# Attention and token mixing on one core: neighbouring heads paired, 128-row loads, and a preparation in which TensorE sums weight halves, pools k and turns q and k of batch 0

## The chip, the core and the metric

The kernel runs on one core of a Trainium2 chip. The metric is the device time in microseconds (us) of one execution. Before the change it is 653.0 us, the median of three runs (652.75 to 656.43). The engines are called as the profile calls them: PE (TensorE, matrix products), PEld (PE's weight loads), DVE (VectorE), ACT (ScalarE), POOL (GpSimd) and SP (SyncE, which issues the transfers here).

## The reference, cut to what matters

```python
# q, k, v: (8 batches, 8 heads, 576 tokens, 64); all float32
k_p = k.reshape(8, 8, 72, 8, 64).mean(axis=3)      # 576 tokens pooled to 72
v_p = v.reshape(8, 8, 72, 8, 64).mean(axis=3)
scores = 0.125 * q @ k_p.transpose(0, 1, 3, 2)
attn = softmax(scores)                             # sum + 1e-9 as divisor
x = concat_heads(attn @ v_p)                       # (8, 576, 512)

theta = x @ w_theta                                # 512x512
zr, zi = x * cos(theta), x * sin(theta)
y = w_tok_r @ zr + w_tok_i @ zi                    # 576x576 each, over the tokens
u = x + y
out = u + relu(u @ w_ch)                           # 512x512
```

The four weights (`moe_w_theta`, `moe_w_tok_r`, `moe_w_tok_i`, `moe_w_ch`) are stored as float64, and the kernel reads them as pairs of 32-bit words. q, k, w_theta and w_tok_i are scaled by 8 in the inputs.

## The kernel before, in words

**Streams and the schedule.** All work is written as small generators, the streams, each of which does one step (a transfer, a multiplication, a copy) between two `yield`s. `SCHEDULE` is a table of 1,882 words written by hand. The kernel walks through it and takes one step of the stream that the word names: `S1.3v` is one step of the stream S1.3, and a letter v, g or a at the end says that DVE, POOL or ACT does it (`pick()` returns the letter). Each engine runs its instructions in the order of the words, so a step that waits holds up everything behind it on its engine.

**Number formats.** A product with weights is made three times in PE's float32r format: each matrix is split into a high part (rounded to float32r) and a low part (the rest), and high x high, low x high and high x low are added in one bank of PSUM. Names in h and l are such pairs: th/tl (w_theta), WTh/WTl (token weights, transposed), chh/chl (w_ch), zh/zl, uh/ul, xh/xl, eh/er (attention).

**Weights.** `to_f32` (L268 to L296) makes float32 from the two words of a float64: seven elementwise steps, the last of which adds the high part t and the small rest s on the engine that the letter names. `channel_weights` (streams h for w_theta, c for w_ch) loads 128 rows in two transfers of 64 (L308, the rows in the order of the paired heads), converts them, and splits the sum into two parts (the low one at L328). `token_weights` (streams w) do the same for 128 rows of w_tok_r or w_tok_i, into one of three buffers `t`; `turn_weights` (W) transposes the blocks of 128x128 on PE (L379, L388, L389) and splits them into WTh and WTl.

**One batch.** The streams of batch b, in the order in which its work flows:
- k, v: loads. K, V: sums over 8 tokens, on DVE and POOL (`pool_sum`, L405 and L410); only v of batch 0 is summed on PE (`pool_on_pe`, L459 and L461), which then holds the sums in PSUM.
- K (`keys`): transposes of the pooled k (L469, L477), copied into kpT.
- Q (`queries`): half of the heads per step, four transfers (L496) that bring blocks of 32 columns, then one stream transpose on DVE (L503).
- S (`soften`, five tiles of 128 tokens): scores on PE (L580), maximum on DVE (L610), exponential on ACT (L618), normalised weights en (L641, L650). Two heads share one multiplication. From batch 2 on, the turned attention weights come back through 32 transfers per batch (L725).
- X: attention times v on PE (L772) into xT. T (five tiles): x is split into xh and xl (xl at L788), theta on PE (L795, bank pt), cosine and sine and the products on ACT and DVE (L799 to L832, L801 and L824 among them), and a transpose of x on PE (L805, px).
- Z: z split into zh and zl (L846). M (`mix`): y on PE (L859), u on DVE (L865). F (`final`): the closing multiplication on PE (L887), ReLU and sum on DVE (L893), and the transfers out.

M and F work on the 576 tokens in two halves of `HALF = S // 2` = 288. Tokens and channels meet in pairs of heads c and c + 2 of each group of four, so the channel order inside the kernel isn't that of the output, and the weights' rows and columns are loaded and split by views that undo this:

```python
    def rows_paired(w):
        return w.rearrange("(j h c d) n -> j c h d n", j=2, h=2, c=2)
```

What decides who waits is thus three things: the table's order on each engine, the landing of the transfers, and how soon a buffer is free again. `EARLY` is 2 (the first two batches turn their attention weights on PE), `V_ON_PE` is 1.

## Time and profile before

| Profiled execution | |
|---|---|
| its time | 655.2 us |
| its span | 653.4 us |
| mean granted TensorE clock | 0.968 |
| PE busy | 593.4 us (91%), 3,891 instructions |
| PEld busy | 544.5 us (83%) |
| DVE busy | 498.2 us (76%), 987 |
| ACT busy | 315.4 us (48%), 675 |
| POOL busy | 303.8 us (47%), 342 |
| chain that ended last | PE 56%, DVE 21%, ACT 9%, DMA 4%, SP's queue 4% |
| DMA | 57.82 MB, 243,991 packets, 232,032 of them under 512 bytes |

The runs without a profile took 656.43, 652.75 and 653.0 us. The share of busy time is a mean over the whole span: PE is busy for 91% of it, yet the first slices of the page show it at 0 to 5 tenths. The preparation (weights, attention of batches 0 and 1) takes about the first 100 us; after it, mixing of one batch runs beside the attention of the next. An instruction's row gives start, duration, engine, line, output<-inputs, and in brackets what ended the wait before it.

### The profile page before, as it was taken

The numbers are of one execution on the slowest core, as the hardware profiler recorded it, in microseconds if no ns is written. First come the engines' busy times: TensorE is split into PE (matmuls) and PEld (weight loads), VectorE is DVE, ScalarE is ACT, GpSimd is POOL, SyncE is SP. The second block draws the span as 40 slices with busy tenths as digits, with TensorE's granted clock in tenths as the row PEclk, the third lists the DMA queues.
The fourth block names the chain that finished last, engine by engine and source line by source line (L and its number), as shares of the span: only waits on it lengthen the run. The fifth ranks groups of instructions, "written<-read, shape, count | busy, mean of one in ns | idle before, by whom it ended". The sixth has DMA issues, their size and how long they took to land.

```text
span 653.4 us, 11040 instructions
## 1 busy us (share of the span) xinstructions
PE 593.4 (91%) x3891; PEld 544.5 (83%) x3891; DVE 498.2 (76%) x987; ACT 315.4 (48%) x675; POOL 303.8 (47%) x342
## 2 busy tenths in 40 slices
PE   0567988999779989999999999999999999999996
PEld 0444568998569988999899989997999989999996
DVE  3879898898687798868898787788877898556424
ACT  2485574767682446424852565316642473155010
POOL 3122342145656856566355474746524516332640
PEclk9985888999989999999999999999999999999999
DMA  9995311247456524826354236641455031402204
GB/s 187 210 246 146 99 42 34 65 87 146 105 96 129 109 59 92 153 39 131 66 104 73 74 73 122 109 93 28 96 90 108 12 62 27 78 1 37 38 1 73
DMA packets 243991, 57.82 MB, mean 88 GB/s; under 512 B 232032, under 2 KB 232544, under 8 KB 243936
## 3 DMA queue, kind: packets, MB, share of 16 engines
q1 hardware_dynamic: 243936, 57.11, 44.2%
q8 instruction: 31, 0.51, 0.3%
q14 instruction: 24, 0.20, 0.1%
HBM read 37.81 MB, written 9.44 MB: 72 GB/s over the span
## 4 chain that ended last, share of the span: by engine, by line
PE 56%; DVE 21%; ACT 9%; DMA 4%; SPq 4%; issue 3%; POOL 2%; DVEq 0%; ACTq 0%; POOLq 0%
PE py L859 27%; PE pf L887 11%; PE pt L795 9%; PE pv L772 5%; PE s L580 3%; SPq L725 2%; DVE mx L610 2%; DMA WTh_st<-in_moe_w_theta_dram 2%; DVE g L801 1%; DVE z L824 1%; PE px L805 1%; ACT g L820 1%; DVE e L625 1%; DVE oT L893 1%; DVE eraw L746 1%
## 5 line engine op out<-in xcount | busy, mean ns | idle before, releaser
L859 PE MATMUL py<-WTh,zh 128*128 128x288 f32 x576 | 88.2, 300 | 1.3 <-DVE xT L865 0.7
L859 PE MATMUL py<-WTl,zh 128*128 128x288 f32 x576 | 88.1, 298 | 0.0
L859 PE MATMUL py<-WTh,zl 128*128 128x288 f32 x576 | 86.9, 298 | 0.0
L859 PEld LDWEIGHTS py<-WTh,zh 128*128 128x128 f32 x576 | 81.3, 192 | 2.3 <-DVE zh L175 1.0
L859 PEld LDWEIGHTS py<-WTl,zh 128*128 128x128 f32 x576 | 81.2, 191 | 0.1
L859 PEld LDWEIGHTS py<-WTh,zl 128*128 128x128 f32 x576 | 79.8, 190 | 0.6 <-DVE xT L865 0.2
L865 DVE TENSOR_TENSOR xT<-py,xT 128x288 f32<-128x288 f32 x64 | 28.5, 448 | 43.5 <-PE py L859 43.0
L580 PE MATMUL s<-kpT,qT 128*128 128x144 f32 (+1 forms) x320 | 49.6, 301 | 6.5 <-DVE e L625 3.2
L872 POOL TENSOR_TENSOR ul<-xT,uh 128x288 fp32r<-128x288 f32 x36 | 31.9, 893 | 45.0 <-ACT uh L173 36.3
L580 PEld LDWEIGHTS s<-kpT,qT 128*128 128x128 f32 (+1 forms) x320 | 43.8, 190 | 9.7 <-issue 3.7
L795 PE MATMUL pt<-th,xh 128*128 128x512 f32 x160 | 47.1, 417 | 3.6 <-ACT xh L173 1.2
L846 POOL TENSOR_TENSOR zl<-z,zh 128x1152 fp32r<-128x1152 f32 x14 | 38.4, 2744 | 23.7 <-ACT zh L173 23.1
L173 ACT CAST uh<-xT 128x288 fp32r<-128x288 f32 x32 | 13.6, 430 | 72.0 <-DVE xT L865 72.0
L795 PE MATMUL pt<-th,xl 128*128 128x512 f32 x160 | 45.4, 407 | 2.8 <-POOL xl L788 2.8
L887 PE MATMUL pf<-uh,chh 128*128 128x288 f32 x256 | 46.6, 304 | 1.2 <-DVE oT L893 1.2
L887 PE MATMUL pf<-ul,chh 128*128 128x288 f32 x256 | 44.8, 295 | 0.1
L799 ACT ACTIVATE g<-pt,c_magic 128x512 f32<-128x512 f32 x38 | 26.1, 687 | 38.8 <-PE pt L795 32.6
L795 PE MATMUL pt<-tl,xh 128*128 128x512 f32 x160 | 44.8, 403 | 0.0
L629 ACT ACTIVATE e<-e 128x576 f32<-128x576 f32 (+1 forms) x30 | 20.6, 686 | 50.0 <-DVE e L625 49.8
L788 POOL TENSOR_TENSOR xl<-xT,xh 128x512 fp32r<-128x512 f32 x26 | 34.2, 1319 | 22.3 <-ACT xh L173 11.7
L887 PE MATMUL pf<-uh,chl 128*128 128x288 f32 x256 | 44.3, 295 | 0.0
L795 PEld LDWEIGHTS pt<-th,xl 128*128 128x128 f32 x160 | 31.2, 196 | 10.6 <-POOL xl L788 3.6
(224 smaller groups left out, 1395.9 us busy)
## 6 DMA issues: line engine op xcount, KB each, us to landing
qsst<-in_q_dram SPq DMA_DIRECT2D x60, 144.0 KB, 3.3
out_dram<-R SPq DMA_DIRECT2D x112, 72.0 KB, 2.0
kpst<-in_k_dram SPq DMA_DIRECT2D x30, 256.0 KB, 4.0
vpst<-in_v_dram SPq DMA_DIRECT2D x28, 256.0 KB, 3.9
eraw<-G SPq DMA_DIRECT2D x96, 60.0 KB, 2.1
eraw<-G SPq DMA_DIRECT2D x96, 40.0 KB, 2.0
WTh_st<-in_moe_w_theta_dram SPq DMA_DIRECT2D x8, 256.0 KB, 7.8
wcraw<-in_moe_w_ch_dram SPq DMA_DIRECT2D x8, 256.0 KB, 4.0
```

The lines of the kernel that those rows point to most:

```text
L173: nc.scalar.copy(out, src)
L580: nc.tensor.matmul(scs[c // 2][:n, 2 * SP * (c % 2) : 2 * SP * (c % 2 + 1)], qT[:, c, t0 : t0 + n], kpT[:, c, :], start=True, stop=True,)
L629: nc.scalar.activation(e[:n], e[:n], AF.Exp, scale=scale)
L772: nc.tensor.matmul(pv[:, :gn], l, r, start=i == 0, stop=i == len(terms) - 1)
L788: ENG[pick()].tensor_tensor(xl, xT[:, :, o], f32(xh), ALU.subtract)
L795: nc.tensor.matmul(pt, l[:, c, :], r[:, c, :], start=i == 0, stop=i == 11)
L799: nc.scalar.activation(g, pt, AF.Identity, bias=c_magic)
L846: ENG[pick()].tensor_tensor(zl, z[:, :, o], f32(zh), ALU.subtract)
L859: nc.tensor.matmul(py[:, :HALF], l[:, kk, :], r[:, kk, t], start=i == 0, stop=i == 3 * NK - 1)
L865: nc.vector.tensor_tensor(u, py[:, :HALF], u, ALU.add)
L872: ENG[pick()].tensor_tensor(ul[:, c, t], u, f32(uh[:, c, t]), ALU.subtract)
L887: nc.tensor.matmul(pv[:, :HALF], l[:, kk, o], uhl[r][:, kk, t], start=i == 0, stop=i == 11)
```

## The change

Four things are changed in the preparation and one in the later loops; the schedule is rewritten throughout.

1. **Neighbouring heads are paired** (heads 2c and 2c + 1 in column block c). The inner channel order is then that of the output. Weights are loaded 128 rows at a time in one transfer instead of two of 64, k in loads of 128 rows of the flattened pools; the small part of en is one multiplication instead of two; the q of batches 1 to 7 comes in 8 transfers per half instead of 4.
2. **float64 halves are summed on PE.** `to_f32` leaves the high part t and the small rest `last` apart. For w_theta PE multiplies both by an identity into one bank (L316 and L317), and the two scaled parts th and tl are read from there. For the token weights the transpose of t and a product of `last` with the identity (`turned`) meet in the bank of the turned block. The sums for w_ch stay elementwise. The token weights have two buffers for t and two for `last`, and one for the step between.
3. **Batch 0's k is pooled on PE** (`K_ON_PE = 1`) and copied out of the bank.
4. **Batch 0's q is loaded by tokens**, in five tiles, and transposed on PE (`queries_on_pe`, `Q_ON_PE = 1`), then copied to qT.
5. **M and F cut the 576 tokens at 256** (256 and 320) instead of 288 and 288.

```diff
-    HALF = S // 2
+    PARTS = ((0, 256), (256, 320))
...
+    identr = const([P, P], F32R, "identr")
+    nc.vector.tensor_copy(identr, ident)
...
     def to_f32(raw, t, s, last=None):
...
-        nc.vector.scalar_tensor_tensor(s, lo.bitcast(U32), step, s, ALU.mult, ALU.mult)
-        yield
-        if scale:
-            nc.vector.scalar_tensor_tensor(t, t, scale, s, ALU.mult, ALU.add)
-        else:
-            ENG[pick()].tensor_tensor(t, t, s, ALU.add)
+        last = s if last is None else last
+        nc.vector.scalar_tensor_tensor(last, lo.bitcast(U32), 2.0**-52, s, ALU.mult, ALU.mult)
         yield
...
@@ channel_weights @@
-        for hh in range(2):
-            nc.sync.dma_start(raw[64 * hh : 64 * hh + 64], rows_paired(w)[c // 2, c % 2, hh])
+        nc.sync.dma_start(raw, w[P * c : P * c + P])
...
+        sum_ = bank([P, DM], *bank_of(c))
+        nc.tensor.matmul(sum_, ident, t, start=True, stop=False)
+        nc.tensor.matmul(sum_, identr, last, start=False, stop=True)
+        yield
+        if pick() == "a":
+            nc.scalar.activation(hi[:, c, :], sum_, AF.Copy, scale=scale)
+        else:
+            nc.vector.tensor_scalar(hi[:, c, :], sum_, scale, None, ALU.mult)
+        yield
+        nc.vector.scalar_tensor_tensor(
+            lo[:, c, :], sum_, scale, f32(hi[:, c, :]), ALU.mult, ALU.subtract
+        )
...
@@ token_weights @@
-            wbufs["t"] = [wa[:, 0 : 2 * S], wa[:, 2 * S :], wb[:, 0 : 2 * S]]
-            wbufs["s"] = [wb[:, 2 * S : 3 * S], wb[:, 3 * S :], wc]
+            wbufs["t"] = [wa[:, 0 : 2 * S], wa[:, 2 * S :]]
+            wbufs["s"] = [wb[:, 0 : 2 * S], wb[:, 2 * S :]]
...
@@ turn_weights @@
+        def turned(out, rows, cols):
+            t, s = wts[m]
+            nc.tensor.matmul(
+                out, t[rows, cols], ident[rows, rows], is_transpose=True, start=True, stop=False
+            )
+            nc.tensor.matmul(out, s[rows, cols], identr[rows, rows], start=False, stop=True)
...
-                    nc.tensor.transpose(pt[:, i - i0, :], src[:, P * i : P * i + P], ident)
+                    turned(pt[:, i - i0, :], every, slice(P * i, P * i + P))
...
+    def queries_on_pe(b, m):
...
+        nc.sync.dma_start(
+            st[:n].rearrange("p (h d) -> p h d", d=D),
+            q[b, :, t0 : t0 + n].rearrange("h s d -> s h d"),
+        )
+        yield
+        pq = bank([P, NC, P], "tp" if m % 2 else "px", f"pq{b}_{m}")
+        for c in range(NC):
+            nc.tensor.transpose(pq[:, c, :n], st[:n, P * c : P * c + P], ident[:n, :n])
+        yield
+        copy(pick(), qTs[b][:, :, t0 : t0 + n], pq[:, :, :n])
...
-        t = slice(HALF * hf, HALF * hf + HALF)
+        t0, n = PARTS[hf]
+        t = slice(t0, t0 + n)
```

The table of the schedule begins differently:

```diff
-k0.0 K0.0v K0.0g k0.2 K0.2g k0.1 K0.1v K0.1v K0.1g w0.0 w0.0 w0.0 w0.0 K0.0g K0 w0.0 w0.0 h0 h2 h0 h2 h0 h0 h2
+k0.0 w0.0 w0.0 w0.0 w0.0 w0.0 k0.1 K0.0 K0.0v h0 h0 h1 K0.1 K0.1a K0 K0a h0 h0 h0 h0 h0 h0 h0v h2 h2 h2 Q0.0
```

How it moves the instructions is shown at three places. In the rows, a line number is that of the kernel in question (the lines from 300 on have moved by 4 to 43), the names are those of the program with a running number at the end, and x4 stands for four like instructions in a row.

First PE at the very start of the program. Before:

```order
L469 MATMUL pk0_120<-ident_66,kp0_99 64x128 x4
L477 MATMUL pkr0_147<-ident_66,kpr0_104 64x64
L580 MATMUL s0_0_171<-kpT_82,qT0_151 128x144 x4
L580 MATMUL s0_1_0_197<-kpT_82,qT0_151 128x144 x2
L580 MATMUL s0_1_1_198<-kpT_82,qT0_151 128x144 x2
L459 MATMUL pvp0_228<-early_95,ident_66 128x128 x16
L461 MATMUL pvp0_228<-vprst0_246,ident_66 64x64 x8
L580 MATMUL s0_2_264<-kpT_82,qT0_151 128x144 x4
```

And PE at the same place now (kpp0 is the bank of the pooled k, ths0 that of the summed w_theta, pq0 that of a tile of q):

```order
L483 MATMUL kpp0_110<-kpst0_0_98,ident_66 128x128 x8
L483 MATMUL kpp0_110<-early_97,ident_66 128x128 x8
L494 MATMUL pk0_137<-ident_66,kp0_119 64x128 x4
L316 MATMUL ths0_150<-WTh_st_122,ident_66 128x512
L317 MATMUL ths0_150<-WTl_st_125,identr_71 128x512
L544 MATMUL pq0_0_160<-ident_66,qsst0_0_158 128x128 x4
L485 MATMUL kpp0_110<-kprst0_168,ident_66 64x64 x8
L504 MATMUL pkr0_179<-ident_66,kpr0_120 64x64
L623 MATMUL s0_0_182<-kpT_84,qT0_157 128x144 x4
L544 MATMUL pq0_1_197<-ident_66,qsst0_0_158 128x128 x4
```

Ahead of the first scores there now stand the pooling of k, the sum of the first tile of w_theta and the transposes of one tile of q; each tile of scores follows its own tile of q instead of all of q.

Second, POOL while the tiles of batch 1 are rotated (xl1_3 is the low part of the fourth tile of x of batch 1, kpst3_0 the first load of k of batch 3, whose sum is kp3). Before:

```order
L788 TENSOR_TENSOR xl1_2_1693<-xT1_1283,xh1_2_1692 128x512
L405 TENSOR_TENSOR kpst3_0_1653<-kpst3_0_1653 128x2x256
L405 TENSOR_TENSOR kpst3_0_1653<-kpst3_0_1653 128x2x128
L410 TENSOR_TENSOR kp3_1721<-kpst3_0_1653 128x128
L788 TENSOR_TENSOR xl1_3_1728<-xT1_1283,xh1_3_1727 128x512
L175 CAST xh1_4_1741<-xT1_1283 128x512
L788 TENSOR_TENSOR xl1_4_1742<-xT1_1283,xh1_4_1741 128x512
```

And POOL now:

```order
L826 TENSOR_TENSOR xl1_2_1698<-xT1_1359,xh1_2_1697 128x512
L409 TENSOR_TENSOR vpst2_1_1720<-vpst2_1_1720 128x2x256
L409 TENSOR_TENSOR vpst2_1_1720<-vpst2_1_1720 128x2x128
L414 TENSOR_TENSOR vp2_1529<-vpst2_1_1720 128x128
L175 COPY xT1_1359<-xT1_1359 128x4x64
L826 TENSOR_TENSOR xl1_3_1712<-xT1_1359,xh1_3_1711 128x512
L175 CAST Vh_88<-vp2_1529 64x4x64 x2
L577 TENSOR_TENSOR Vl_856<-vp2_1529,Vh_88 64x4x64 x2
L409 TENSOR_TENSOR kpst3_0_1815<-kpst3_0_1815 128x2x256
L409 TENSOR_TENSOR kpst3_0_1815<-kpst3_0_1815 128x2x128
L414 TENSOR_TENSOR kp3_1705<-kpst3_0_1815 128x128
```

The low part of the fourth tile stands ahead of the sum of batch 3's first k load instead of behind it; between the third and the fourth tile there stands now a sum of v of batch 2.

Third, PE at that place (pt is theta, px the transposed x, s2 scores of batch 2, pf0 the closing multiplication of batch 0). Before:

```order
L795 MATMUL pt1_3_1762<-th_92,xl1_3_1728 128x512 x4
L580 MATMUL s2_2_1792<-kpT_82,qT2_1290 128x144 x4
L805 MATMUL px1_3_1804<-ident_66,xT1_1283 128x128 x4
L795 MATMUL pt1_4_1815<-th_92,xh1_4_1741 128x512 x4
L795 MATMUL pt1_4_1815<-tl_93,xh1_4_1741 128x512 x4
L795 MATMUL pt1_4_1815<-th_92,xl1_4_1742 128x512 x4
L469 MATMUL pk3_1839<-ident_66,kp3_1721 64x128 x4
```

And PE now:

```order
L833 MATMUL pt1_3_1785<-th_94,xl1_3_1712 128x512 x4
L843 MATMUL px1_3_1801<-ident_66,xT1_1359 128x128 x4
L623 MATMUL s2_2_1827<-kpT_84,qT2_1260 128x144 x4
L927 MATMUL pf0_3_0_1851<-uh0_1006,chh_905 128x256 x4
L927 MATMUL pf0_3_0_1851<-uh0_1006,chl_906 128x256 x4
L927 MATMUL pf0_3_0_1851<-ul0_1007,chh_905 128x256 x4
L833 MATMUL pt1_4_1872<-th_94,xh1_4_1810 128x512 x4
L833 MATMUL pt1_4_1872<-tl_95,xh1_4_1810 128x512 x4
L833 MATMUL pt1_4_1872<-th_94,xl1_4_1811 128x512 x4
L843 MATMUL px1_4_1888<-ident_66,xT1_1359 128x128 x4
```

Two pieces of the closing multiplication of batch 0, which stood ahead of this place, now stand between the last tiles of batch 1 (pf0_3_1 a few rows further down).

More of the change, by code (lines that the diff above doesn't have):

```diff
@@ L387, in turn_weights @@
             for i in range(4):
-                nc.tensor.transpose(pt[:, i, :], src[:, P * i : P * i + P], ident)
-            nc.tensor.transpose(pt[0:64, 4, :], src[:, 4 * P : S], ident)
+                turned(pt[:, i, :], every, slice(P * i, P * i + P))
+            turned(pt[0:64, 4, :], every, slice(4 * P, S))
             yield
@@ L440, in pool @@
             yield
+            if name == "kp":
+                main, rem = pooled[name, b]
+                if ("kq", b) not in pooled:
+                    pooled["kq", b] = [
+                        work([P, NC, D], F32, "kp", f"kp{b}"),
+                        work([64, D], F32, "kpr", f"kpr{b}"),
+                    ]
+                if j < 2:
+                    copy(pick(), pooled["kq", b][0][:, 2 * j : 2 * j + 2, :], main[:, 2 * j : 2 * j + 2, :])
+                else:
+                    copy(pick(), pooled["kq", b][1], rem)
+                yield
             return
@@ L465, in keys @@
     def keys(b):
-        km = pooled["kp", b][0]
+        what = "kq" if b < K_ON_PE else "kp"
+        km = pooled[what, b][0]
         pk = bank([P, NC, P], "tp", f"pk{b}")
```

377 lines of the change are left out of this document (189 added, 188 removed).

## The prediction

> **What bounds the kernel now.** I read the page first: engine shares and the slices.
>
> ```profile
> span 653.4 us, 11040 instructions
> ...
> PE 593.4 (91%) x3891; PEld 544.5 (83%) x3891; DVE 498.2 (76%) x987; ACT 315.4 (48%) x675; POOL 303.8 (47%) x342
> ...
> PE   0567988999779989999999999999999999999996
> ...
> PEclk9985888999989999999999999999999999999999
> ```
>
> PE is busy 593.4 of 653.4 us, and from the thirteenth slice on it is full until the tail. So after the preparation almost only PE's own work counts, and the idle time of PE to be won lies at the left and in one dip. Which engine paces the left part is read from the stretches (columns as in the first line; the last three are granted clock, DMA share and GB/s).
>
> ```profile
> core 0: us, PE busy (x) PEld busy (x) DVE busy (x) ACT busy (x) POOL busy (x), PEclk, DMA share, GB/s
> 0.00:27.07 27.07, 4.04 (x15) 3.02 (x16) 14.14 (x31) 6.82 (x13) 7.69 (x16) 1.00 0.96 194
> 27.07:46.50 19.43, 14.11 (x93) 12.39 (x93) 15.79 (x43) 15.77 (x78) 3.86 (x4) 0.97 1.02 250
> 46.50:70.50 24.00, 19.71 (x55) 12.01 (x54) 21.75 (x47) 10.64 (x36) 5.36 (x5) 0.52 0.53 132
> 70.50:101.40 30.90, 25.25 (x119) 18.62 (x120) 28.40 (x50) 24.13 (x41) 12.53 (x11) 0.92 0.25 63
> 101.40:163.00 61.60, 60.51 (x429) 57.38 (x428) 53.55 (x117) 38.73 (x146) 21.80 (x33) 0.98 0.41 88
> 163.00:196.00 33.00, 23.96 (x122) 19.52 (x121) 25.38 (x48) 25.89 (x40) 19.51 (x27) 0.89 0.52 100
> ```
>
> I cut at 27.07, where DVE takes the first maximum of scores, at 101.40, where the first mix of tokens is under way, and at 46.50 and 70.50, between which the clock was granted at 0.52. Up to 27.07 DMA is the fullest (0.96). From there to 101.40 DVE is busy 15.79 + 21.75 + 28.40 = 65.94 of 74.33 us and PE 14.11 + 19.71 + 25.25 = 59.07: **DVE is the pacer of the preparation, with PE close behind** and partly at half clock. PE leaves idle 23.0 us up to 27.07, 15.3 us up to 101.40, and 9.0 us in the dip from 163 to 196.
>
> **The change part by part.** First the start.
>
> ```profile
> 5.78 0.69 DVE L405 TENSOR_TENSOR kpst<-kpst 128x512 f32<-128x512 f32 x1 [3.67 <-DMA kpst<-in_k_dram]
> ...
> 12.48 0.71 ACT L277 ACTIVATE wsrc_b<-wraw 128x576 f32<-128x576 f32 x1 [9.03 <-DMA wraw<-in_moe_w_tok_r_dram]
> ...
> 16.66 0.66 ACT L277 ACTIVATE WTl_st<-WTh_st 128x512 f32<-128x512 f32 x1 [1.48 <-DMA WTh_st<-in_moe_w_theta_dram]
> ...
> 25.70 3.25 PE L580 MATMUL s<-kpT,qT 128*128 128x144 f32 x12 [2.20 <-DVE qT L503]
> 27.07 0.76 DVE L610 TENSOR_REDUCE mx<-s 128x8 f32<-128x576 f32 x1 [0.85 <-PE s L580]
> ```
>
> The first k tile (0.52 MB) has landed at 5.78. Before 16.66 there have landed also the rest of k (0.66 MB), 0.59 MB of w_tok_r and two tiles of w_theta (1.05 MB): 2.3 MB in 10.9 us, 0.21 MB per us. The first scores wait for a stream transpose of all of q of batch 0 (1.18 MB) on DVE. In the new order they need k, 0.59 MB of w_tok_r, three tiles of w_theta (1.57 MB) and 0.26 MB of q: 3.6 MB, of which 3.08 after the first tile, so an estimate of 5.8 + 3.08 / 0.21 = 20.5 us, and some 2 us of chain behind it (sum on PE, copy, transpose, copy, 4 matmuls). First maximum at 22.5 instead of 27.07: **-4.5**.
>
> Then DVE's work. The groups by form (busy us, mean ns, idle before):
>
> ```profile
> L503 DVE STREAM_TRANSPOSE qT<-qsst 128x1152 f32<-128x1152 f32 x15 | 20.5, 1367 | 0.0
> L405 DVE TENSOR_TENSOR kpst<-kpst 128x512 f32<-128x512 f32 x3 | 2.1, 685 | 3.7 <-DMA kpst<-in_k_dram 3.7
> L294 DVE SCALAR_TENSOR_TENSOR WTl_st<-WTl_st 128x512 f32<-128x512 f32 x4 | 2.7, 676 | 0.0
> L296 DVE TENSOR_TENSOR wcts<-wcts 128x512 f32<-128x512 f32 x4 | 2.8, 689 | 0.1
> L801 DVE SCALAR_TENSOR_TENSOR g<-g,pt 128x512 f32<-128x512 f32 x38 | 25.7, 677 | 18.2 <-ACT g L799 18.0
> L328 DVE TENSOR_TENSOR tl<-WTl_st,th 128x256 fp32r<-128x256 f32 x6 | 2.2, 409 | 0.0
> ```
>
> I counted DVE's instructions up to the first zl of both programs. Gone: 2 stream transposes of q (2.7); 3 of the 4 widest k and v adds at 0.685 and the narrower ones behind them, taken as 0.7 of it each (2.1 + 1.4 = 3.5); 4 scaled sums at L294 (2.7); 2 of 3 sums at L296 (1.4); 2 of 4 xl and 1 of 4 en, which go to POOL (three instructions over 512 columns, 2.1 at 0.69). New: 4 copies out of PSUM, three of 512 columns and one of 128 (2.3, priced like L801, which reads PSUM too), 4 subtractions for tl at 0.677 and 2 scalings for th, for 6 of 0.409 (4.1 less 2.5, +1.6). Sum -12.4 + 3.9 = -8.5 us. Most of it (6 us: the q transposes, the k sums, one sum and one scaled sum of weights) stands ahead of the first maximum, and is in the -4.5 already. The rest is **-2.5**, in full while DVE is the pacer, nothing once PE is.
>
> What PE gets for it, and the new cut of the tokens:
>
> ```profile
> 28.74 5.23 PE L459 MATMUL pvp<-early,ident 128*128 128x128 f32 x32
> ...
> 305.01 1.36 PE L859 MATMUL py<-WTh,zh 128*128 128x288 f32 x9
> 306.21 0.31 PE L772 MATMUL pv<-eh,Vh 128*128 128x320 f32 x1
> ...
> 306.65 0.31 PE L772 MATMUL pv<-er,Vr 96*128 96x320 f32 x1
> 306.80 1.14 PE L580 MATMUL s<-kpT,qT 128*128 128x144 f32 x8
> 307.69 0.79 PE L887 MATMUL pf<-uh,chh 128*128 128x288 f32 x4
> ...
> 311.30 0.60 PE L805 MATMUL px<-ident,xT 128*128 128x128 f32 x4
> 311.65 0.39 PE L772 MATMUL pv<-eh,Vh 128*128 128x320 f32 x1
> ...
> 336.12 0.28 PE L772 MATMUL pv<-eh,Vh 128*128 128x256 f32 x1
> ...
> 336.47 0.28 PE L772 MATMUL pv<-er,Vr 96*128 96x256 f32 x1
> ```
>
> From start to start, 9 matmuls of 288 columns take 1.20 us (0.133 each), 3 of 320 take 0.44 (0.147), 3 of 256 take 0.35 (0.117). 0.147 + 0.117 is 0.264, twice 0.133 is 0.266: cutting 576 tokens at 256 instead of 288 costs **0**. The k sum is the v sum of L459 again: 5.2 us and some for the remainder, but in the 23.0 us in which PE idles. Twenty q transposes at 0.35 / 4 are 1.8 us. A float32 pass over 144 columns is one of two records at 0.89 / 8 = 0.111, so four sums of w_theta over 512 columns take 2 x 0.111 x 512 / 144 = 0.79 each and a single float32r pass of about 0.24 (0.147 and three more steps of 0.030 per 64 columns): 4.1 us. The second matmul behind each of 41 blocks of the token weights (float32r, 128 columns) isn't in this trace: from below it costs like a transpose, 0.0875, from above like a whole float32 product of 144 columns, 0.222: 3.6 to 9.1 us. I take 5, near the transpose, the row with the same block and the same identity. Beyond 27.07 that is some 10 us more (8.5 to 15) for 15.3 us of idle time; most of the idle time is spread in small waits for DVE, so I charge **+3** (bounds 0 and 13).
>
> One more term is POOL. The two rows overlap:
>
> ```profile
> 77.25 1.58 POOL L296 TENSOR_TENSOR wsrc_b<-wsrc_b,wsrc_c 128x576 f32<-128x576 f32 x1 [9.48 <-DVE wsrc_c L291]
> ...
> 77.46 1.69 DVE L289 TENSOR_SCALAR wsrc_b<-wsrc_a 128x576 int32<-128x576 int32 x1
> ...
> 174.49 2.19 POOL L405 TENSOR_TENSOR kpst<-kpst 128x512 f32<-128x512 f32 x2 [3.46 <-DMA kpst<-in_k_dram]
> ...
> 177.17 1.28 POOL L788 TENSOR_TENSOR xl<-xT,xh 128x512 fp32r<-128x512 f32 x1
> ...
> 178.51 1.98 PE L795 MATMUL pt<-th,xl 128*128 128x512 f32 x4 [2.48 <-POOL xl L788]
> ```
>
> The DVE instruction at 77.46 has groups' fellows of 0.46 and took 1.69, while POOL added the halves of the weights. These adds leave POOL, so up to 1.2 us of DVE goes with them; other POOL adds take their place near there, so I credit **-0.5** (0 to -1.2). The Trainium skill, "SBUF — State Buffer", section "Who interferes with whom", says that the two engines share one pair of ports which is locked for a whole instruction, so that the later one blocks fully; by that rule all of the 1.2 us goes, and the trace agrees in this one pair of rows.
>
> The other three rows are in the dip. PE waits 2.48 us for xl of the fourth tile of batch 1, which stands on POOL behind the sum of the first k tile of batch 3, and that waits 3.46 us for its load. In the new order xl stands ahead of that k sum, and the last two pieces of the closing multiplication of batch 0 (12 matmuls at 0.117 and 12 at 0.147, 3.2 us) now come behind it, where PE waited. Together 5.7 us; the dip holds 9.0 us of PE idle time, and the clock of 0.89 some 3 more. Waits for DVE stay (25.38 of 33.00 busy), so I take **-5** (0 to -12).
>
> ```profile
> 135.23 2.61 SPq L496 DMA_DIRECT2D qsst<-in_q_dram  x4
> ```
>
> The q of batches 1 to 7 comes in 8 transfers for each half instead of 4. One issue takes 2.61 / 4 = 0.65 us of SP, so the 32 blocks of the turn behind it on the queue, or the outputs, start up to 2.6 us later. SP has no computing to do and waits more than it issues, so **0**; without that cover 2.6 us per batch, 18 us in all at worst, would show as waits of PE on eraw. One multiplication for the small part of en instead of two, and loads in 128 rows instead of twice 64, take work from engines that are not full after 163: 0.
>
> Sum against the profiled execution, 655.2 us (span 653.4 and 1.8 around it): -4.5 - 2.5 + 3 - 0.5 - 5 = -9.5, so 645.7. The median of the runs is 653.0, 2.2 lower; a like run of the new kernel is **643 us**.
>
> **The clock.** In the stretch of 24 us at 0.52 PE was busy 19.71 us: busy time by the profile does not bring the clock back, and the work there would take some 10 us less at full clock. The new order puts more of PE's work ahead of this stretch and into it. If that keeps the clock up, the time from 63 to 70 shrinks, where PE was the pacer; if not, each added microsecond counts twice. The skill's page "TensorE: Matmul & The Clock Gate", "Part 4: PE-mode transpose", says that transposes don't count as busy for the clock in the way products do; by that rule most of what is added here (q and the token weights) can't lift it, and the second of these is the outcome: the slower rival below. No row separates the kinds of work, so the trace neither agrees nor disagrees.
>
> **The rivals.**
> - *PE becomes the pacer at half clock, slower.* Place: the turning of the token weights and of tokens of batch 0, 46 to 101 us. Price: the upper 15 us of added work at half clock are up to 30, less the 15.3 us of idle time, less 5 us of earlier start and 2.5 of DVE's: +8; nothing from the dip: 661. It decides from where the work added beyond 27.07, at the granted clock, exceeds the 15.3 us. For it: 0.52. Against: PE waited for DVE even there (24.00 - 19.71 = 4.3 us).
> - *The gain is taken back, no change.* The weights' conversion now has two target buffers instead of three and waits for PE's turning, and PE's two matmuls for each block stretch the round trip; this returns the -4.5 of the start, and the dip gives 3 instead of 5: 649 to 650. For it: DVE and PE are both near full from 46 on. This is also the case in which the new order does not cure the dip.
> - *Both come whole, much faster.* The clock stays up (-3.5, half of the 7 us from 63 to 70), DVE's 8.5 us show in full instead of 7, PE's additions fill idle time (0 instead of +3), and the dip gives 10: 643 - 3.5 - 1.5 - 3 - 5 = 630.
>
> **How the numbers follow.** Forecast 0.50 (638 to 648), much faster 0.16, no change 0.23, slower 0.11. The range leaves out the slower rival and the lower half of the much faster one: 630 to 654. A measurement of this kernel tells about 1% (6.5 us) from no change: its three runs spread over 3.7 us. Faster by over 1% is below 646.5: 0.16 and four fifths of 0.50 with a little of the third case, 0.58. Within 1%: the rest of the forecast, most of the third case and a small part of the slower one: 0.34. Slower by over 1%, above 659.5: 0.08.
>
> **What would show it.** Right: a first maximum near 22 to 23 us; the first mix between 94 and 98 instead of near 101; no wait of PE for xl behind a k load; less than 5 us of PE idle in the dip, now some 6 us earlier; matmuls of 256 and 320 columns with 0.264 for a pair. Wrong: the clock at half far beyond 70 us; float32r matmuls of 128 columns at 0.2 us or more; PE waiting for the copies out of the bank of the turned weights; a new dip elsewhere, since the whole order after 163 is another and I read it only where before lost time.

## The result: 630.1 us, and where the profile after differs

The changed kernel took 630.11 us (median of four runs, 629.45 to 630.52), the kernel before 654.71 in the same comparison (652.75 to 657.3): a ratio of 0.9621, 95% interval 0.9578 to 0.9664. The forecast was 643 with a range of 630 to 654. The direction was right, the size was not: 24.6 us came, some 10 had been counted. Medians and spreads, here and in the experiments, leave out an execution that took over 1.5% longer than the fastest of its kernel (one of e13, one of e16).

The page of the changed kernel, its span, busy times, and the rows of PE and of the clock in 40 slices:

```profile
span 628.7 us, 11243 instructions
...
PE 595.1 (95%) x4012; PEld 549.7 (87%) x4012; DVE 495.4 (79%) x952; ACT 300.9 (48%) x637; POOL 303.6 (48%) x340
...
PE   6789979999899989999999999999999999999996
...
PEclk9899979999899999999999999999999999999999
```

PE is busy as long as before (595.1 against 593.4 us), with 121 instructions more; what went is its idle time, 60.0 to 33.6 us. The half clock of the fourth slice is gone. To see where, I cut both traces at the same four events: the first maximum of scores on DVE, the first mix of batch 0, that of batch 1, and the end (columns as in the stretches of the prediction). Before, then after:

```profile
27.07:100.80 73.73, 58.48 (x263) 42.42 (x263) 65.34 (x137) 49.95 (x154) 21.75 (x20) 0.81 0.54 135
100.80:193.25 92.45, 82.32 (x540) 74.75 (x539) 76.78 (x164) 62.93 (x182) 40.93 (x60) 0.96 0.45 92
193.25:653.40 460.15, 448.61 (x3077) 424.33 (x3077) 341.93 (x658) 195.74 (x328) 233.46 (x247) 0.99 0.40 74
```

```profile
0.00:17.01 17.01, 11.41 (x70) 9.84 (x71) 10.68 (x23) 6.61 (x13) 3.33 (x9) 1.00 0.91 292
17.01:85.33 68.32, 57.19 (x330) 42.84 (x328) 65.22 (x122) 51.99 (x158) 21.91 (x27) 0.95 0.53 150
85.33:173.84 88.51, 82.17 (x540) 75.35 (x539) 80.05 (x166) 56.29 (x157) 41.94 (x52) 0.96 0.41 94
173.84:628.70 454.86, 444.28 (x3077) 421.68 (x3077) 339.42 (x643) 186.02 (x310) 236.45 (x253) 1.00 0.40 75
```

The start is 10.1 us shorter (17.01 against 27.07), the preparation 5.4, the stretch with the dip 3.9, the rest 5.3: together 24.7. In the start DMA is as full as before (0.91 against 0.96), but it moves 292 GB/s, not 194. In the preparation **DVE is busy for as long** (65.22 against 65.34 us) in less time: its idle time fell from 8.4 to 3.1 us, and that is the gain. What DVE waited for in the preparation, by its waits (total, times, longest), before and after:

```profile
DVE g L801 <- ACT g L799: 3.2, 2, 2.1
DVE Vr L518 <- PE pvp L461: 2.8, 1, 2.8
DVE mx L610 <- PE s L580: 1.5, 2, 0.8
```

```profile
DVE wsrc_a L280 <- ACT wsrc_a L278: 1.3, 1, 1.3
...
DVE mx L653 <- PE s L623: 0.2, 1, 0.2
```

The second and third wait are for PE: for the pooled rest of v and for scores. The first is for ACT, which had itself waited 5.58 us for PE, for theta (pt) of the first tile; 2.11 us of it stand in the second row. Theta of this tile took from 63.4 to 68.9 us before, at half clock, and from 49.8 to 52.8 us after, at full clock. Before, then after:

```profile
68.95 0.69 ACT L799 ACTIVATE g<-pt,c_magic 128x512 f32<-128x512 f32 x1 [5.58 <-PE pt L795]
69.67 0.69 DVE L801 SCALAR_TENSOR_TENSOR g<-g,pt 128x512 f32<-128x512 f32 x1 [2.11 <-ACT g L799]
```

```profile
53.64 0.67 DVE L839 SCALAR_TENSOR_TENSOR g<-g,pt 128x512 f32<-128x512 f32 x1
```

Of these three waits only 0.2 us for scores is left. In the last stage PE's busy time fell by 4.3 us (448.61 to 444.28). About 2.7 of them lie at its very beginning, where the half clock behind the dip reached into the first mix of batch 1. Before, then after:

```profile
193.25:199.10 5.85, 5.85 (x24) 5.85 (x25) 4.12 (x3) 3.86 (x8) 1.86 (x3) 0.50 0.33 53
```

```profile
173.84:179.70 5.86, 5.86 (x45) 5.86 (x46) 5.51 (x9) 2.62 (x5) 4.02 (x3) 1.00 0.47 100
```

In the same time PE did 24 matmuls before and does 45 now; at 5.86 / 45 = 0.13 us each, the 21 are an estimate of 2.7 us.

### The profile page after: what moved, and what is told of

The parts are those of the page before. It is cut to its first block, busy times and chain, and to the rows that moved or that the text cites. A ratio compares the mean times of both kernels' runs of the same rounds, so it can differ in the third digit from the quotient of the medians.

```text
span 628.7 us, 11243 instructions
## 1 busy us (share of the span) xinstructions
PE 595.1 (95%) x4012; PEld 549.7 (87%) x4012; DVE 495.4 (79%) x952; ACT 300.9 (48%) x637; POOL 303.6 (48%) x340
## 4 chain that ended last, share of the span: by engine, by line
PE 67%; DVE 15%; ACT 5%; SPq 5%; DMA 3%; issue 3%; POOL 1%; DVEq 0%; POOLq 0%; ACTq 0%
PE py L898 32%; PE pt L833 11%; PE pf L927 10%; SPq L763 5%; PE pv L810 5%; PE s L623 4%; PE px L843 2%; DMA eraw<-G 1%; DVE mx L653 1%; DVE en L684 1%; DVE e L668 1%; DVE z L862 1%; PE wt L363 1%; DVE g L839 1%; DMA wraw<-in_moe_w_tok_r_dram 1%
## 5 line engine op out<-in xcount | busy, mean ns | idle before, releaser
L898 PE MATMUL py<-WTl,zh 128*128 128x256 f32 (+1 forms) x576 | 87.9, 298 | 0.0
L898 PE MATMUL py<-WTh,zh 128*128 128x256 f32 (+1 forms) x576 | 86.7, 299 | 0.5 <-ACT zh L173 0.5
L898 PE MATMUL py<-WTh,zl 128*128 128x256 f32 (+1 forms) x576 | 84.3, 294 | 0.0
L904 DVE TENSOR_TENSOR xT<-py,xT 128x256 f32<-128x256 f32 (+1 forms) x64 | 28.4, 443 | 36.8 <-PE py L898 36.6
L672 ACT ACTIVATE e<-e 128x576 f32<-128x576 f32 (+1 forms) x30 | 20.6, 686 | 59.6 <-DVE e L668 51.0
L927 PE MATMUL pf<-uh,chh 128*128 128x320 f32 (+1 forms) x256 | 47.3, 307 | 1.6 <-DVE oT L933 1.6
L173 ACT CAST uh<-xT 128x256 fp32r<-128x256 f32 (+1 forms) x28 | 11.9, 431 | 71.3 <-DVE xT L904 71.3
L911 POOL TENSOR_TENSOR ul<-xT,uh 128x320 fp32r<-128x320 f32 (+1 forms) x38 | 33.9, 904 | 23.6 <-DVE uh L175 13.3
L927 PE MATMUL pf<-ul,chh 128*128 128x320 f32 (+1 forms) x256 | 44.8, 297 | 0.0
L927 PE MATMUL pf<-uh,chl 128*128 128x320 f32 (+1 forms) x256 | 44.6, 296 | 0.0
L927 PEld LDWEIGHTS pf<-uh,chh 128*128 128x128 f32 x256 | 38.3, 192 | 3.5 <-DVE oT L933 2.1
```

The costliest lines, as they stand in the source:

```text
L672: nc.scalar.activation(e[:n], e[:n], AF.Exp, scale=scale)
L898: nc.tensor.matmul(py[:, :n], l[:, kk, :], r[:, kk, t], start=i == 0, stop=i == 3 * NK - 1)
L904: nc.vector.tensor_tensor(u, py[:, :n], u, ALU.add)
L911: ENG[pick()].tensor_tensor(ul[:, c, t], u, f32(uh[:, c, t]), ALU.subtract)
L927: nc.tensor.matmul(pv[:, :n], l[:, kk, o], uhl[r][:, kk, t], start=i == 0, stop=i == 11)
```

## The experiments

Each kernel ran beside the kernel before on the same chip (four chips in all), whose medians there were 654.8 to 655.6. The changed kernel has its 630.1 from the comparison above, against 654.7; a difference to it of 1 us or less can therefore come from the comparison. The table gives the median, and from one profile each the first maximum and the length of the three stages above.

| kernel | median us | first maximum | to first mix | mix 0 to mix 1 | to the end |
|---|---|---|---|---|---|
| before | 654.7 | 27.1 | 73.7 | 92.4 | 460.1 |
| after | 630.1 | 17.0 | 68.3 | 88.5 | 454.9 |
| e1 no second product | 632.6 | 16.6 | 70.2 | 88.3 | 455.8 |
| e2 cut at 288 | 631.8 | 16.5 | 67.0 | 88.4 | 458.5 |
| e3 64-row loads | 638.3 | 20.3 | 68.8 | 90.8 | 456.6 |
| e4 q in 128-byte runs | 632.1 | 17.2 | 67.9 | 88.5 | 456.7 |
| e5 k pooled on DVE | 636.9 | 20.6 | 69.9 | 88.6 | 456.1 |
| e6 before, PE work added | 670.1 | 26.8 | 87.2 | 92.4 | 458.7 |
| e7 before, xl ahead of k | 656.8 | 26.6 | 75.1 | 94.6 | 459.4 |
| e8 after, PE work added | 643.9 | 17.0 | 81.3 | 86.8 | 456.3 |
| e9 before, waits filled | 654.7 | 26.4 | 75.1 | 92.5 | 459.6 |
| e10 after, pf0_3_0 earlier | 630.0 | 16.8 | 68.3 | 88.1 | 456.5 |
| e11 after, waits filled | 628.9 | 16.4 | 67.7 | 87.4 | 453.2 |
| e12 all of q first | 634.9 | 20.4 | 67.8 | 88.5 | 456.4 |
| e13 two transfers by columns | 634.2 | 18.8 | 66.7 | 87.3 | 454.8 |
| e14 v in 128 rows | 728.4 | 17.2 | 96.4 | 102.4 | 510.7 |
| e15 e3, e5 and e12 together | 641.8 | 25.8 | 67.7 | 90.1 | 456.1 |
| e16 e10, e11 and e14 | 732.2 | 16.2 | 97.9 | 102.9 | 513.5 |
| e17 sums off PE | 654.6 | 18.1 | 91.8 | 88.1 | 454.7 |
| e18 e10 and e11 | 629.6 | 16.7 | 68.4 | 87.6 | 457.6 |

**Loads: e3, e4, e13.** The loads of w_theta, w_ch and k in two halves of 64 rows:

```diff
-        nc.sync.dma_start(raw, w[P * c : P * c + P])
+        for hh in range(2):
+            r0 = P * c + 64 * hh
+            nc.sync.dma_start(raw[64 * hh : 64 * hh + 64], w[r0 : r0 + 64])
```

> The changed kernel with the loads of w_theta, w_ch and k (not its remainder) in two transfers of 64 rows each instead of one of 128, the same bytes in the same order. Theory A (the rows per transfer set the rate of the first 20 us, 284 GB/s against 183): the rate of the first 17 us falls towards 200 GB/s, the first maximum of scores comes at 20 us or later instead of 17.0, and the time rises by 2 to 5 us. Theory B (the rate is set by the short runs of q, not by rows): the rate stays at 270 or more, the first maximum at 17 to 18, the time within 1 us of 630.1.

Theory A in kind: the rate of the first 17 us fell from 292 to 242 GB/s. It cost 8.2 us, the most of the parts that were undone alone. The stretch from 4 to 12 us, before, after, and with halves of 64 rows:

```profile
4.00:12.00 8.00, 0.00 (x0) 0.00 (x0) 1.81 (x3) 0.00 (x0) 2.29 (x4) 1.00 1.04 211
```

```profile
4.00:12.00 8.00, 7.06 (x36) 6.53 (x37) 4.28 (x16) 1.65 (x3) 0.00 (x0) 1.00 1.01 367
```

```profile
4.00:12.00 8.00, 4.66 (x20) 4.40 (x21) 2.37 (x12) 1.30 (x2) 0.00 (x0) 1.00 1.02 292
```

The last two columns are DMA's share and GB/s: the engines of the DMA are full in all three, and move 211, 367 and 292 (before, q in 128-byte runs is among it). A busy share does not tell the rate. The first maximum came 3.3 us later, and the stage with the dip was 2.2 us longer. Of that, 0.9 us are waits of PE for a sum of k and for an xl (0.6 and 0.3, neither of which the changed kernel has). The larger wait is one of 1.9 us (0.5 without the halves) at 122 us, for DVE, which converts w_ch then; w_ch is loaded in halves too. The Trainium skill, "DMA: Bandwidth & Descriptors", section "Rules for kernel authors", advises against two transfers to disjoint halves of the partitions and for one of 128; this run agrees, with 8.2 us.

Shorter runs of q:

```diff
+        for d0 in (0, 32):
             nc.sync.dma_start(
-                st[:n].rearrange("p (h d) -> p h d", d=D),
-                q[b, :, t0 : t0 + n].rearrange("h s d -> s h d"),
+                st[:n].rearrange("p (h d) -> p h d", d=D)[:, :, d0 : d0 + 32],
+                q[b, :, t0 : t0 + n].rearrange("h s d -> s h d")[:, :, d0 : d0 + 32],
             )
```

> The changed kernel with each load of q of batch 0 split in two transfers of 128-byte runs (the first and the last 32 columns of each head) instead of one of 256-byte runs; the same bytes. Theory A (short runs set the rate of the first loads): the stretch in which q lands moves fewer GB/s, the first maximum comes 1 to 3 us later than 17.0, and the time rises by 1 to 4 us. Theory B (runs of this length do not matter, rows do): first maximum at 17 to 17.5 and the time within 1 us of 630.1.

From 12 to 20 us the rate fell from 253 to some 180 GB/s, but the first maximum moved by 0.2 us only, since the first scores need one tile. That is theory B's first maximum; the time, 2.0 us more, is within the spread of the runs (629.6 to 634.7).

The same number of transfers as in e3, but 128 rows and half the columns each (k alike, by its two blocks of 128 pools):

```diff
-        nc.sync.dma_start(raw, w[P * c : P * c + P])
+        for x in (0, DM):
+            nc.sync.dma_start(raw[:, x : x + DM], w[P * c : P * c + P, x : x + DM])
```

> The changed kernel with the loads of w_theta, w_ch and k (not its remainder) in two transfers each, as in the run with 64 rows, but cut across the columns: 128 rows and half the bytes per row. Theory A (rows per transfer set the rate): first maximum at 17 to 18 us and the time within 1.5 us of the changed kernel. Theory B (the number of transfers, that is their issue on SP, sets it): first maximum at 19 to 20.5 us and the time 4 to 8 us above, as with 64 rows (638.3).

Inconclusive: the five runs spread from 629.5 to 637.6. The profiled one took 629.5, with the first maximum at 18.8, between the two theories. The loads of k landed 2.9 us after issue (median; 3.6 in e3), so rows count, but the number of transfers isn't excluded as a second cause.

**The other parts of the start: e5, e12, e15.** Batch 0's k on DVE again (in the step in which PE pooled):

```diff
-            pool_on_pe(b, name, j, st)
+            w = POOL * D // 2
+            while w > D:
+                nc.vector.tensor_tensor(st[..., 0:w], st[..., 0:w], st[..., w : 2 * w], ALU.add)
+                w //= 2
+            nc.vector.tensor_tensor(dst, st[..., 0:w], st[..., w : 2 * w], ALU.add)
```

> The changed kernel with batch 0's k pooled on DVE again (three adds for each of the two 128-row loads and for the rest, in the step in which PE pooled before), order and loads unchanged. Theory A (the early start comes from PE's pooling, since DVE was full up to the first maximum): the first maximum comes 2 to 4 us later than 17.0 and the time rises by 2 to 4 us. Theory B (the start is set by when the loads land; DVE waits there, 6 us of 17 idle): the first maximum moves by less than 1 us and the time by less than 1.5 us.

Theory A, and more than it said: 6.8 us, 3.6 of it ahead of the first maximum and 1.6 in the preparation. All five tiles of q ahead of the first scores, in the steps of the first tile:

```diff
     def queries_on_pe(b, m):
+        if m:
+            yield
+            yield
+            yield
+            return
...
+        for i, st in enumerate(sts):
...
+            copy("v" if i % 2 == 0 else "a", qTs[b][:, :, P * i : P * i + n], pq[:, :, :n])
```

> The changed kernel with all five tiles of batch 0's q loaded, transposed on PE and copied ahead of the first scores instead of tile by tile; the same transfers and instructions. Theory A (the early start comes in part from needing only the first tile of q): the first maximum comes 3 to 6 us later than 17.0, and the time rises by 2 to 5 us. Theory B (with the faster loads all of q is there early enough): the first maximum within 2 us of 17.0 and the time within 1.5 us.

4.8 us, 3.4 of it at the start: theory A. The three together:

> The changed kernel with three parts undone together: 64-row loads of w_theta, w_ch and k, batch 0's k pooled on DVE, and all of batch 0's q ahead of the first scores. Undone alone they cost 8.2, 6.8 and 4.8 us. Theory A (they add): 19 to 20 us above 630.1, near 650, the first maximum near 27, and only some 5 us of the gain come from all else (order, sums on PE, cut of the tokens). Theory B (they overlap, since each is hidden where another ends last): 8 to 13 us above, 638 to 643, and the new order brings half of the gain.

Theory B: 11.6 us, less than the 19.8 of the three alone, so they overlap. The first maximum goes back to 25.8, so **8.8 of the 10.1 us of the start are these three parts**. What is left against the kernel before in the same comparison is 13.6 us, some 1.3 of it at the start and the rest in the other stages: the preparation stays at 67.7 and does not need the three.

**What PE's work in the preparation is worth: e1, e8, e6, e17.** Without the second product behind the 41 blocks:

```diff
-            nc.tensor.matmul(out, s[rows, cols], identr[rows, rows], start=False, stop=True)
```

> The changed kernel without the second product behind each of the 41 transposed blocks of the token weights; the small rest of these weights is left out of the sum, and everything else, the steps that compute it included, stays. Theory A (these products are work in the sense of the clock, and the preparation runs at full clock because of them): the granted clock falls to about 0.5 somewhere between 44 and 76 us, as it did in the kernel before, and the time is 2 to 8 us above the 630.1 of the changed kernel although 41 instructions are gone. Theory B (the products are only a cost, and the clock stays for other reasons): the clock stays at 1.00 there and the time is 0 to 4 us below 630.1; 41 x 0.107 = 4.4 us of PE if PE paces, nothing if DVE does.

With three more of them ahead of each block:

```diff
+            for _ in range(3):
+                nc.tensor.matmul(out, s[rows, cols], identr[rows, rows], start=True, stop=True)
```

> The changed kernel with three more products of 128 columns ahead of each of the 41 transposed blocks of the token weights (the small rest times the identity into the place that the transpose then overwrites), 123 in all and by the 0.107 us of the one that is there already 13 us of PE. Theory A (PE paces the preparation from 44 to 85 us): the time rises by 8 to 13 us. Theory B (DVE paces it, and PE's waits take the added work): the time rises by 0 to 5 us; together with the run without the second product it tells what PE's work there is worth.

Taking 41 products away brought nothing. It took 2.5 us more (630.7 to 634.6), and the clock was 0.93 from 46.5 to 70.5, at half from 49.5 to 52.9 where the changed kernel has 1.00: theory A's signs, but small. PE, with 2.3 us less to do, waited 7.2 us for DVE's low parts of the token weights, where it waits 5.4. Adding 123 cost 13.8, 0.112 each, their whole length, as theory A said. The preparation in e8:

```profile
17.10:98.40 81.30, 70.24 (x452) 56.65 (x450) 70.07 (x125) 52.06 (x158) 21.94 (x27) 0.95 0.46 130
```

13.1 us of busy PE more, 13.0 us of time more: DVE, which paced before, now waits 7.3 us for copies out of the bank of the turned weights, and is busy for 4.9 us more (three instructions more in the stretch, others longer). I read this as one chain of the two engines, balanced to a few us, in which PE's work has no price below that point and its whole length above it; that the clock also moved in e1 is the other reading of its half, and isn't excluded. Added work on the kernel before had a price too (the second `extra` stands ahead of each turning step):

```diff
+    def extra(out, times):
+        for i in range(4 * times):
+            o = out[:, P * (i % 4) : P * (i % 4) + P]
+            nc.tensor.matmul(o, identr, identr, start=True, stop=True)
...
+        if b == 0:
+            extra(pt.rearrange("p c x -> p (c x)"), 3)
```

> The kernel before with 12 products of an identity with itself (float32r, 128 columns) added on PE ahead of the transposes of each attention tile of batch 0 and ahead of each step that turns token weights, 156 in all; they write a bank that the transposes then overwrite. Theory A (the half clock from 45 to 70 us comes from PE being too little at work from 35 to 45, and it costs the preparation time): the granted clock stays near 1.00 from 46 to 70, and the time falls by 2 to 8 us below the 654.8 of the kernel before although PE does more. Theory B (the half clock is a symptom of a preparation that DVE paces): the clock rises or not, and the time stays within 2 us or rises by up to 8 (156 x 0.05 to 0.1 us of added PE work, less what lies in waits).

14.4 us more, and the clock went to 0.67 from 46.5 to 70.5, not to 1.00: neither theory foresaw that 156 small products would cost 0.09 us each in a stage with 15.3 us of idle PE. The sums off PE:

```diff
+        nc.gpsimd.tensor_tensor(t, t, f32(last), ALU.add)
...
+        nc.vector.tensor_tensor(t, t, f32(last), ALU.add)
```

> The changed kernel with the sums of the float64 halves off PE: the token weights' on POOL in the last step of their conversion (9 adds, some 1.6 us each in the kernel before), w_theta's on DVE (4 adds of 0.69 us), and no second product behind the transposes, no sums of w_theta in PSUM. Theory A (prediction: these sums are PE work at a price, 4.1 + 5 us of which 3 show): the time falls by 0 to 3 us. Theory B (DVE paces the preparation, busy for 65.2 of 68.3 us, and what the sums take from DVE, and POOL's adds from beside it, is worth more than PE's time): the time rises by 4 to 8 us: 2.8 us of DVE for w_theta, and the wait of the transposes for POOL's 9 x 1.6 us where it isn't hidden.

24 us more than the changed kernel, beyond both theories, but it does not price the sums: the adds stand on POOL ahead of work that PE waits for (6.9 us for the adds, 6.3 for an xl behind one), a place that this order was not written for. In it the low part of the first tile of w_theta and both parts of the second are split from a buffer that by then holds another tile; only its time is read.

**The clock: e9, e11.** Products of the identity on PE only where it waited, in the kernel before:

```diff
+        if b == 0 and m == 1:
+            extra(pt.rearrange("p c x -> p (c x)"), 14)
...
+        if b == 0 and g0 == 0 and c == 0:
+            extra(pv, 16)
```

> The kernel before with products of an identity with itself (float32r, 128 columns, 0.128 us each in the run before last) put on PE only where it waited: 14 ahead of the transposes of the second attention tile (a wait of 2.01 us at 38.4) and 16 ahead of the first product of attention with v (a wait of 2.13 us at 43.1, behind which the clock was granted at 0.5). Theory A (a wait of PE of some 2 us or more is followed by half clock, and the half clock costs time because PE's own work counts in the preparation): the clock stays at 1.00 from 46 to at least 59 us, where the next long wait (3.20 us) ends, and the time falls by 2 to 6 us although nothing is taken away. Theory B (the clock falls for another reason, or the lost speed lies beside DVE's work): the clock falls at about 45 as before, or the time stays within 1.5 us.

The timeline of PE from 43 to 53 us, before and with the fill:

```profile
42.79 0.30 PE L682 MATMUL per<-ident,spare 128*64 128x128 f32 x1
45.21 0.96 PE L772 MATMUL pv<-eh,Ve 128*128 128x256 f32 x2 [2.13 <-ACT eh L173]
```

```profile
43.42 1.98 PE L204 MATMUL pv<-identr 128*128 128x128 f32 x16
45.91 0.70 PE L783 MATMUL pv<-eh,Ve 128*128 128x256 f32 x2 [0.51 <-ACT eh L173]
...
50.90 0.66 PE L683 MATMUL pe<-ident,spare 128*128 128x128 f32 x4 [1.88 <-DVE spare L648]
...
52.00 0.91 PE L783 MATMUL pv<-eh,Ve 128*128 128x256 f32 x2 [0.27 <-ACT xT L173]
```

The same two products take 0.96 us behind a wait of 2.13 and 0.70 behind the fill: here the clock follows PE's waits. It fell at the next one (1.88 us for DVE) instead, and was also lower from 35 to 39 us (0.57), behind a wait of 2.44; over the preparation it rose only from 0.81 to 0.83. The time did not move: 654.7. But theta of the first tile, for which DVE waits, still ran at half clock:

```profile
64.11 2.07 PE L806 MATMUL pt<-th,xh 128*128 128x512 f32 x4 [0.82 <-ACT er L173]
```

So e9 raised the clock only where DVE did not wait for it, and does not tell what full clock at theta is worth. The fill in the changed kernel, behind the turned fourth block row:

```diff
+                if m == 3:
+                    extra(bank([P, 512], "mm", f"fill{i0}", bufs=2), 12 if i0 else 18)
```

> The changed kernel with products of an identity with itself (float32r, 128 columns) on PE behind the two groups of transposes of the fourth block row of the token weights, 18 and 12, where PE waited 2.56 and 1.88 us for DVE and the clock fell to 0.5 from 83 to 89 us. Theory A (the fill keeps the clock, and the turning of the last block row and the first mix run at full clock): granted clock 1.00 from 80 to 92 and the time lower by 1.5 to 3 us. Theory B (the clock falls all the same, or the fill delays the last transposes): the time within 1 us or above.

628.9 (626.5 to 635.4), 1.2 us less than the changed kernel, within the spread; the clock fell all the same, at 79 us instead of 82.

**The dip: e7, e10.** In the kernel before, one word of the table moved, so that POOL sums the k load behind both xl:

```diff
-K3.0g S2.0 T1.3a T1.3g X1.2.3v ... T1.4g T1.3
+S2.0 T1.3a T1.3g X1.2.3v ... T1.4g K3.0g T1.3
```

> The kernel before with one word of its schedule moved: POOL sums the first k load of batch 3 behind the low parts xl of the fourth and fifth tiles of batch 1 instead of ahead of them. Theory A (prediction: that wait of 2.48 us makes half of the dip): no wait of PE for xl behind the load, PE idle between 163 and 196 us falls from 9.0 to 5 to 7 us, and the time falls by 2 to 5 us. Theory B (PE then waits for DVE or for the load at the next tile, or for the k sum at the keys of batch 3): the idle time only moves, and the time stays within 1.5 us.

Theory B. The waits of PE in the dip of this kernel:

```profile
PE pk L448 <- POOL kp L389: 3.6, 1, 3.6
PE pt L774 <- DVE g L780: 2.1, 2, 1.9
...
PE pt L774 <- POOL xl L767: 0.3, 1, 0.3
```

The wait for xl is gone (2.8 to 0.3 us), and the keys of batch 3 now wait 3.6 us for the second k sum, which itself waited 2.46 us for its load. In the changed kernel neither wait is there; its own longest wait in this stage is another:

```profile
PE px L843 <- DVE z L862: 2.4, 1, 2.4
```

A piece of the closing multiplication put ahead of that wait, by one word of the table:

```diff
-T1.3 F0.2.1 T1.4a T1.3 k3.0 ... T1.3a T1.3 F0.3.0 T1.3
+F0.3.0 T1.3 F0.2.1 T1.4a T1.3 k3.0 ... T1.3a T1.3 T1.3
```

> The changed kernel with one word of its schedule moved: the seventh piece of the closing multiplication of batch 0 (pf0_3_0, 12 products) stands ahead of the transposes px1_3, where PE waited 2.35 us for DVE and was at half clock for some 3 us behind it. Theory A (waits of 2 us cost their length and the half clock behind them): PE idle from the first mix of batch 0 to that of batch 1 falls by about 1.5 to 2 us, no half clock there, the time falls by 1.5 to 3.5 us. Theory B (DVE paces this stretch, 31.01 of 33.00 us busy, so PE only waits later): within 1 us of the changed kernel.

630.0, theory B: nothing that the runs can tell.

**The cut of the tokens: e2.**

```diff
-    PARTS = ((0, 256), (256, 320))
+    PARTS = ((0, 288), (288, 288))
```

> The changed kernel with the tokens cut at 288 and 288 again. Theory A (prediction: 0.117 + 0.147 is twice 0.133, the cut costs nothing): within 1 us of 630.1. Theory B (the cut itself brings time: in the two traces the starts of the mix's matmuls are 0.1367 us apart on the mean at 288 columns, 0.1473 and 0.1208 at 320 and 256, 0.0026 less for each of 1,728 matmuls): about 4 to 5 us above, near 635.

631.8, 1.7 us more, within the spread. In the last stage it took 458.5 us, where the thirteen kernels with the new cut and v in 64 rows took 453.2 to 457.6 (mean 455.8) and the four with the old order 458.7 to 460.1. But PE is busy in this stage for 445.53 us in e2, 444.28 in the changed kernel and 448.61 before, so by this profile the cut accounts for 1.3 us of PE's work. The rest of the 3.6 us between e2 and the changed kernel is idle time of PE (12.9 against 10.6), and e18, with the new cut, idles as long (12.9). The cut is worth 1 us or little more, and theory B's 4 to 5 us are not seen.

**v in 128 rows, and all together: e14, e16, e18.** The v loads cut by columns, with the head as the outermost of the source's dimensions:

```diff
-                            "(j c h) (g r) d -> j h g c (r d)", j=2, h=2, r=POOL
-                        )[j, hh],
+                            "(j c h) (g r) d -> j c h g (r d)", j=2, h=2, r=POOL
+                        )[j, c],
```

> The changed kernel with the loads of v, which still come in two transfers of 64 rows each, in two of 128 rows with half the bytes per row; same number, same bytes. Theory A (rows per transfer set the rate): the median time from issue to landing of the v loads falls from 3.7 to 3 us or less, and the time falls by 0 to 3 us (v is needed early for batch 0 only, and its sums stand on POOL beside other work). Theory B: landing and time unchanged within 1 us.

98 us slower, which neither theory had. DMA's share and GB/s in 40 slices from 10 to 60 us:

```profile
DMA  9988411111111113249899711159992211141415
GB/s 313 292 200 186 95 48 52 49 52 52 49 52 49 52 52 106 87 92 336 236 350 274 234 57 66 49 167 369 394 374 69 82 23 41 52 102 52 101 53 117
```

While v is loaded, a tenth of the DMA engines is busy and 50 GB/s move. The Trainium skill, "DMA: Bandwidth & Descriptors", section "Why a DMA increments its semaphore by 16 and not by 1", says that a transfer runs on the largest number of engines, up to 16, that divides the slowest dimension of both sides; here that is the 2 of the heads, and the trace agrees. The other two:

> The changed kernel with the v loads in 128 rows, the seventh piece of the closing multiplication ahead of the transposes px1_3, and the 30 products of an identity that fill PE's waits behind the fourth block row of the token weights. Alone the last two gave 0.1 and 1.2 us against 630.1, within the spread of the runs. Theory A (they add, since they touch different places): 626 to 628.5. Theory B (DVE paces both places): 629 to 631.

> The changed kernel with the seventh piece of the closing multiplication ahead of the transposes px1_3 and the 30 products of an identity that fill PE's waits behind the fourth block row of the token weights. Theory A (they add): 626 to 628.5. Theory B (DVE paces both places and the spread of the runs hides the rest): 629 to 631.

e16 carries the v loads of e14 and tells nothing else. e18 took 629.6 (628.4 to 632.0), theory B: no version is faster than the changed kernel by more than the runs can tell.

## Why the prediction was wrong in size

By the two profiles 24.7 us came where 9.5 had been added up. The 15.2 that were missing are 5.6 at the start, 5.4 in the preparation and 5.3 in the last stage, less 1.1 in the stage with the dip.

- **Start, -4.5: it was -10.1.** The step that failed is "5.8 + 3.08 / 0.21 = 20.5". The rate of 0.21 MB per us was measured on loads of 64 rows (and q in 128-byte runs) and applied to loads of 128. The bytes were right:

```profile
5.78:15.00 9.22, 8.49 (x54) 6.99 (x53) 6.16 (x13) 3.21 (x8) 0.00 (x0) 1.00 1.08 341
```

  With these 0.341 MB per us the same sum gives 14.8, and 16.8 with its 2 us of chain; the maximum came at 17.0 instead of 22.5. The loads "in 128 rows instead of twice 64" were priced at 0 in the paragraph on SP's issues; undone alone they cost 8.2.
- **DVE's work, -2.5 behind the first maximum: it was -0.1** (65.34 to 65.22 us busy); the runs do not show why. Ahead of it DVE's busy time fell by 3.5 (14.14 to 10.68). The 6 of the prediction came behind 4.42 us (13.48 to 7.66), but up to there DVE has 2.4 us more (0.66 to 3.02), which the count left out: the copy of the identity (2.67 us) and longer sums for the mask (2.91 where they took 0.56), while the first load was on its way.
- **PE's added work, +3 with bounds of 0 and 13:** not separable as a sum term. The second products took 0.107 each (13.1 us over the 123 of e8) where 0.0875 to 0.222 was given; 41 of them cost nothing that shows (e1), three times as many cost their whole length (e8). The bounds were right to be wide.
- **The preparation as a whole, -2.5 + 3 - 0.5 = 0: it was -5.4**, DVE's waits for PE. What the sum put at nothing is PE's clock: it rose from 0.81 to 0.95, and PE's busy time fell by 1.3 us (58.48 to 57.19) with some 10 us of work added by the prediction's own count. The prediction had the clock as a case apart ("The clock stays up") and put it at -3.5 with a chance of 0.16. That the clock rose is shown, and that DVE's wait for theta went; that full clock saved this time, and not the new order, is not, since e9 left theta at half clock.
- **Its paragraph on the clock** counts most of what is added, "q and the token weights", as transposes. By its own sum it isn't: the 41 second matmuls, the sums of w_theta and the k sum are products, and the transposes of q are 1.8 us.
- **The dip, -5: it was -3.9, and some 2.7 more in the stage behind it**, where the half clock is gone: together more than forecast. The wait for xl behind the k load is gone as forecast, but the order on POOL alone does not bring the time: in e7 it only moves to the keys, which wait for the k sum. With the new order and 64-row loads both waits come back only as 0.3 and 0.6 us (e3). So the order of all streams matters more than the one word, and how the gain divides between order and loads is open.
- **The cut of the tokens, 0,** and **POOL's adds, -0.5**: the first is right to some 1 us (e2), the second was not isolated.
- **SP's issues, 0:** right, PE has no wait for eraw in the changed kernel. The worst case was added up wrongly: two halves of q per batch, each with 4 transfers more, are 5.2 us per batch and 36 in all, not 2.6 and 18.
- **The rivals.** "Much faster" at 630 was met in its number by luck. Of its reasons the clock and the filled idle time came in the preparation; DVE's 8.5 us (3.6 in all) and 10 us in the dip did not, and it did not have the loads. "PE becomes the pacer at half clock" did not come: the clock was 1.00 from 46.5 to 70.5. What it says of PE's work above DVE's is real all the same (e8). "The gain is taken back" did not come either: the start and the preparation both became shorter.

What stays open: how the 5.4 us of the preparation divide between the new order, the sums on PE and the clock, and some 1.5 us of the last stage, which the spread of this stage over the kernels hides.

## What to carry to other kernels

A rate taken from a trace belongs to the shape of the transfers that made it: a DMA share near 1 does not say that the bytes could not move faster. Price a change of a load's shape by the time of everything that waits for it, not by the busy engines. Where two engines hand work to each other with single buffers, ask for the price of work from both sides: taking 41 products away gave nothing, adding 123 cost all of it.

## What the runs showed of the hardware that I had not expected

- One load of 128 rows against two of 64: 367 against 292 GB/s from 4 to 12 us at the same DMA share (211 before, with q in 128-byte runs among it).
- Transfers whose outermost dimension is 2 moved at 50 GB/s; 32 of them, 4 of batch 0 and 28 others, cost 98 us.
- Half clock behind waits of PE of 2.13 us (before) and 1.88 (e9), and in e1 behind two of only 0.42 and 1.00; behind one of 2.01 (before, at 40.4 us) it did not fall. In the kernel before it stayed at half for 24 us, through stretches in which PE was busy all the time (4.00 of 4 us from 48 to 52):

```profile
44.00:48.00 4.00, 2.79 (x8) 1.55 (x9) 3.93 (x11) 2.93 (x12) 1.41 (x1) 0.69 0.82 129
48.00:52.00 4.00, 4.00 (x13) 2.37 (x11) 4.00 (x12) 3.98 (x20) 0.00 (x0) 0.50 0.90 316
```
